# RetNet retention and a SwiGLU block on one core: later segments' retention in half chunks of 64 tokens instead of whole chunks of 128

## The chip, the core and the metric

The kernel runs on one core of a Trainium2 chip. TensorE (PE in the profile) multiplies into PSUM, which has eight banks here, each 128 partitions by 512 float32 columns. VectorE (DVE), ScalarE (ACT) and GpSimd (POOL) do the element-wise work, and SyncE (SP) issues nearly all DMAs in one ordered queue. The metric is the device time of one execution in microseconds (us). The kernel before took 665.63 us (median of 3 runs, 664.43 to 665.97).

## The reference

```python
q, k, v: (4, 8, 768, 64)            # batch, heads, sequence, head_dim
gamma = 1.0 - 2.0 ** (-5.0 - np.arange(H))
for t in range(S):
    state = gamma * state + einsum('bhd,bhe->bhde', k[:, :, t], v[:, :, t])
    y[:, :, t] = scale * einsum('bhd,bhde->bhe', q[:, :, t], state)
x = y.transpose(0, 2, 1, 3).reshape(B * S, H * D)       # 3072 x 512
g = x @ w_gate; silu = g / (1 + exp(-g)); val = x @ w_val
return (silu * val) @ w_out          # d_ff 1536, weights in float64 words
```

Retention is a recurrence over tokens with one 64x64 state for each head, and can be done by chunks. Inside a chunk, scores of key and query are multiplied by a table of decays and then by the values. What lies before the chunk enters as the query, scaled, times the state at the chunk's start. At the chunk's end the state is decayed and the scaled keys times the values are added.

## The kernel before

**Segments and stages.** The 24 chunks of 128 tokens (4 batches of 6) are worked through in four segments of six chunks. A segment has three pairs, the two chunks of a pair being at the same place in two batches. Each segment goes through an up stage (the gate and value products over 12 slices `f` of the hidden size) and a down stage (72 slots, six for each slice, of three matmuls each, `down`, L917). The first segment's retention stands at the start of the program, and its up stage is `up` (L692), in which the weights are also read from memory, converted from float64 words, split and stored for the later segments. The order of that work is written out by hand in two strings of tokens, `START` and `beside` (L299 and L306): `l` loads a chunk's part, `A` a part of the decay table, `s m o t` are the parts of retention, `U a b c S C T Z` the stages of one up weight, `F Z` those of one down weight, `P` a load for the next segment.

**Retention of segments 1 to 3** is put between the slots of the down stage before it (`down_stage`, L956). I call the three passes loop 1 (down stage of segment 0, in which segment 1's retention is computed) to loop 3. The table `PARTS` (L945 to L950) says before which slot a part of which pair comes. For each pair there are five visits: `s` for heads 0 to 3 and `s` for heads 4 to 7 (`scores_of`, L556), `m` (`mix_own`, L609), `o` (`mix_other`, L620) and `t` (`state2`, L652). The first pair has its two `s` in one visit, and the last chunk of a sequence has no `t`. All of these matmuls go through one helper, `mm` (L552), so the profile shows them as L552.

**How a pair lies on the array.** Every part but the state multiplies with 64 rows and 64 columns, so that four such matmuls have four different quarters of the array. For each head a chunk has three blocks of scores of its four: both halves of the queries against the first half of the keys as one matmul of 128 columns (`low`), and the second half of the queries against the second half of the keys as one of 64 (`high`). The state's matmuls use all 128 rows, 64 columns wide. In all a pair has 48 matmuls of 128 columns and 48 of 64.

**What stands beside it.** `decayed` (DVE) takes scores out of PSUM with the decay table (L574), `scale_q2` scales the queries in place (one chunk on DVE, the other on POOL, L628), `scale_k2` the keys (16 ACT instructions, L639, or POOL), `decay2` the old state (4 on ACT, L650), `keep_state` adds the new sum (L666), `bring_y` copies the result out of PSUM (8 on ACT, L805), and `make_x` splits it for the next up stage. Banks 6 and 7 (`R0`) hold scores, then results, then state sums of a pair, one after another.

**What sets the order.** Each engine's instructions stand in the order of planned times: `at(t, ...)` puts a step at a time, `run` sorts them. The times come from `COST`, from `PASS_U` and `PASS_D`, and from the table `WHEN` (L334), which holds an offset for each step. Loads for the coming retention are put at slots by `LOADS` (L953); `HOME` (L516) says which of five places of the tile `loads` each takes, and so on whose last reader each waits. `UNITS` puts the first up weights of the next segment into the same places.

Of the kernel before, what the change touches and what calls it, by code (L numbers as in the profile page):

```python
# [17 lines left out]
P = 128  # L18
# [31 lines left out]
def tile_retnet_swiglu(  # L50
# [203 lines left out]
    def sums_t(piece, parts=range(3)):  # L254
# [30 lines left out]
        "L": lambda n: load_side(n // 2, n % 2), "h": lambda n: high_side(n),  # L285
# [6 lines left out]
    def do(order):  # L292
        for o in order.split():
# [6 lines left out]
        l0:0 A1 l1:0 l0:3 A0 l0:2 l1:3 s0 l2:0 l2:1 A2 l1:2 l3:0 l3:1 l4:2 l4:0 l2:3 l2:2 s1  # L300
        l3:3 m0 l4:1 K0 U0:0 s2 l3:2 m1 k1 l5:0 Q2 l5:1 V0:0 x0:0 l5:2 t0 l4:3 s3 o2 q3 k2
        x0:1 t1 U1:2 g2 k3 m2 l5:3 a0:1 x0:2 t2 o3 s4 g3 x0:3 m3 x1:0 t3 b0:1 a0:0 c0:1 S0:1
        b0:0 s5 q4 S0:0 c0:0 q5 x1:1 o4 x1:2 x1:3 o5 m4 C0:1 m5 a1 x2:0 C0:0 b1 T0:0 p0 x2:1
        T0:1 T0:2 S1 p1 c1 x2:2 C1
    """
    beside = """  # L306
        U14:8 | x2:3 g4 | U2:0 | T1:0 U15:9 | T1:1 c2 a2 b2 | S2 C2 U3:4 |
        T2:0 U12:6 | g5 c12 U13:7 | T2:1 a3 Z0 a13 T1:2 | U5:0 a12 b3 M0 b12 | c3 S3 Z1 | C3
            T2:2 |
        U4:2 L0 L1 | S12 M1 a5 T3:0 | C12 | F12:0 a4 F12:1 | T3:1 L3 U6:4 b4 c4 S4 T3:2 | b5  # L310
            c6 C4 S5 F12:2 T4:0 |
         | c5 Z2 T4:1 | C5 a6 b13 M2 c13 | S13 a14 b6 T4:2 C13 | h0 Z3 T5:0 b14 T5:1 | S6
            F13:0 F13:1 U7:2 U16:6 U8:0 |
        M3 F12:3 | Z4 S14 T5:2 c7 | a7 F13:2 a15 C6 F13:3 | c14 Z12 b15 U17:7 U9:4 | Z13 b7
            C14 T6:0 F14:0 F14:1 T6:1 | T6:2 |
        S7 C7 | F14:2 a8 | S15 c15 b8 a16 F14:3 | C15 M4 | a17 c8 | F15:0 F15:1 |
        Z5 T7:0 S8 T7:1 C8 M5 b16 | U10:2 T7:2 L2 Z6 | U19:9 U11:0 S16 T8:0 a9 c16 | Z14
            U18:8 | F15:2 c17 | C16 b9 T8:1 F16:0 b17 h1 S9 |
        c9 F16:1 | T8:2 F16:2 C9 S17 | M6 F16:3 | F15:3 C17 T9:0 c10 P2 a10 | b10 U20:6 a18
            k4 F17:0 S10 a19 Z7 U21:7 | T9:1 Z15 F17:1 c18 |  # L320
        a11 M7 | F17:2 U23:5 C10 T9:2 | b18 S18 F17:3 Z9 | c11 b11 T10:0 T10:1 C18 b19 | P1
            F18:0 F18:1 c19 S19 S11 k5 | Z16 |
        a20 F18:2 Z8 a21 | t4 | C19 F18:3 C11 U22:4 c20 P0 M8 | b20 T11:0 F19:0 | b21 F19:1
            S21 T11:1 | T11:2 a23 S20 F19:2 a22 C20 |
        Z17 Z18 T10:2 M9 F20:0 F19:3 | b23 F20:1 c21 Z10 C21 F20:2 Z19 | b22 S22 c22 F21:0 |
            F20:3 S23 t5 c23 C22 | F22:0 | F21:1 Z20 C23 |
        Z11 | F23:0 F21:2 F22:1 F21:3 F22:2 M10 | F22:3 | Z22 F23:1 |  | F23:2 F23:3 |
# [26 lines left out]
        ('h', 6): (-7.31, -2.68, -1.02),  # L354
# [148 lines left out]
    def mix(c):  # L503
        vn, a = chunks[c][2], att.pop(c)
        y, own = y_parts(c)
        for k, (n, i, to) in enumerate(own):
# [7 lines left out]

    spots = [loads[:, ts(i, 512)] for i in range(10)]
    HOME = (2, 3, 4, 0, 1, 2, 3, 4, 0, 1, 4, 0)  # L516
    blocks = [loads[:, ds(i, UNIT)] for i in (2048, 2048 + UNIT, 0)]
    side = [t.rearrange("p (i t) -> p i t", i=2)
            for t in (tab[:, : 2 * TA], kept_vk.rearrange("p a b -> p (a b)")[:, : 2 * TA])]
    kdec_b = tab[:, ds(2 * TA, H)]  # L520
    half = [ds(0, D), ds(D, D)]
# [3 lines left out]
    def load_side(g, m):  # L525
        cols = decays[:, MASK0:QDEC0].rearrange("p (i g t) -> p i g t", i=2, g=2)[:, :, g]
        nc.sync.dma_start(out=side[g][half[m], :, : 2 * P], in_=cols[half[0]])
        if g == 0:
            nc.sync.dma_start(out=kdec_b[half[m]], in_=decays[half[1 - m], ds(KDEC0, H)])

    def high_side(g):

        low, high = (side[g][:, :, c].rearrange("p i (n t) -> p i n t", n=2)
                     for c in (ds(0, 2 * P), ds(2 * P, P)))
        for i in range(2):
            copy(high[:, i], low[:, i, :, :D])

    def load_pair(s, n):
        p, w = divmod(n, 4)
        w = (0, 1, 2, 3)[w]  # L540
        own = [spots[2 * HOME[n] + i] for i in range(2)]
        given.setdefault(p, {})[w] = own
        for i in range(2):
            src = (k_t, q_t, v_n, k_n)[w][seg_chunks(s)[2 * p + i]]
            if w < 2 or i == 0:
                nc.sync.dma_start(out=own[i], in_=src)
            else:
                for m in half:
                    nc.sync.dma_start(out=own[i][m], in_=src[half[m is half[0]]])
# [4 lines left out]
    score_banks = {}  # L554

    def scores_of(p, g, own=(R0, R0 + 1)):  # L556
        score_banks[p, g] = own = [banks[i] for i in own]
        kt, qt = ([pairs(t) for t in given[p][w]] for w in range(2))
        for b in range(2):
            for m in range(2):  # L560
                for r in range(2):
                    x, n = half[r], 2 * g + b
                    mm(own[r][half[m], ts(b, P)], kt[m][x, n, half[0]],
                       qt[m][x, n], b == 0)
        for b in range(2):
            for m in range(2):
                for r in range(2):
                    x, n = half[r], 2 * g + b
                    mm(own[r][half[m], ds(2 * P + D * b, D)],
                       kt[1 - m][x, n, half[1]], qt[1 - m][x, n, half[1]])  # L570

    def decayed(p, g, i):
        att[p, g, i] = tmp[:, ts(2 * g + i, TA)]
        tt(att[p, g, i], score_banks[p, g][i][:, :TA], side[g][:, i], op=mul)  # L574
# [7 lines left out]
    def old(s, p, other):  # L582
        for b in range(2):
            for h in range(2):
                for r in range(2):
                    c, n = (1 - r if other else r), 2 * h + b
                    mm(y_of(n, r, c), state_of(seg_chunks(s)[2 * p + c], 1)[half[r], n],
                       pairs(given[p][1][c])[half[r], n], b == 0 and not other)

    def low(p, first):  # L590
        for i in range(2):
            for b in range(2):
                for h in range(2):
                    for r in range(2):
                        n = 2 * h + b
                        mm(y_of(n, i, r), given[p][2][r][half[r], ts(2 * n + i, D)],
                           att[p, h, i][half[r], ts(b, P)], first and i == b == 0)

    def high(p):
        for i in range(2):  # L600
            for b in range(2):
                for h in range(2):
                    for r in range(2):
                        n = 2 * h + b
                        mm(y_of(n, i, 1 - r, half[1]),
                           given[p][2][1 - r][half[r], ts(2 * n + i, D)],
                           att[p, h, i][half[r], ds(2 * P + D * b, D)])

    def mix_own(s, p):  # L609
        ci = seg_chunks(s)[2 * p] % NCK  # L610
        if ci:
            old(s, p, False)
        low(p, ci == 0)
# [6 lines left out]
    def mix_other(s, p):  # L620
        high(p)
        if seg_chunks(s)[2 * p] % NCK:
            old(s, p, True)

    def scale_q2(p, i):
        t = pairs(given[p][1][i])
        if i:
            pool(t, t, qdec, op=mul)  # L628
        else:
            both(t, t, qdec, mul)  # L630

    def scale_k2(p, i):
        kd = given[p][3][i].rearrange("p (h d) -> p h d", h=H)
        dec = kdec_b if i else kdec
        if p == 2 and i == 0:
            pool(kd, kd, dec[:, :, None].to_broadcast([P, H, D]), op=mul)
            return
        for h in range(H):
            act(kd[:, h], kd[:, h], AF.Copy, scale=dec[:, ds(h, 1)])  # L639

    def new_states(s, p):
        ci = seg_chunks(s)[2 * p] % NCK
        new, was = (states[:, (ci + o) % 2] for o in range(2))
        return ci, new, was, banks[R0].rearrange("p (c n e) -> p c n e", c=2, n=NP)

    def decay2(s, p):
        ci, new, was, st = new_states(s, p)
        if ci:
            for n in range(NP):
                act(new[:, :, n], was[:, :, n], AF.Copy, scale=gdec[:, ds(n, 1)])  # L650

    def state2(s, p):  # L652
        ci, new, was, st = new_states(s, p)
        for c in range(2):
            vn, kd = given[p][2][c], given[p][3][c]
            for n in range(NP):
                for i in range(2):
                    h = ts(2 * n + i, D)
                    mm(st[half[i], c, n], kd[:, h], vn[:, h], c == n == 0)

    def keep_state(s, p):
        ci, new, was, st = new_states(s, p)
        if ci == 0:
            copy(new, st)
        else:
            tt(new, new, st, op=add)  # L666
# [278 lines left out]
    CYCLE = [("s", 0, 0), ("s", 1, 4), ("m", 0, 9), ("o", 0, 12), ("t", 0, 16)]  # L945
    STARTS = (2, 22, 41)
    PARTS = {}
    for p, b in enumerate(STARTS):
# [167 lines left out]
```

## Time and profile before

| what | us |
|---|---|
| median of three runs | 665.63 |
| the profiled execution, its own time | 665.63 |
| its span, first to last instruction | 663.8 |
| start, before the first up-stage matmul | 0 to 27 |
| up stage of segment 0 | 27 to 140 |
| loop 1, 2, 3 (down stage with the next segment's retention) | 140 to 209, 297 to 366, 454 to 521 |
| up stages of segments 1, 2, 3 | 209 to 297, 366 to 454, 521 to 607 |
| last down stage, no retention | 610 to 657 |

The profile is one execution. Where a matmul of float32 is recorded it stands as two records, so "x32" of L552 is 16 matmuls. Busy time of an engine is the union of its instructions. The chain of waits goes back from the last instruction to what released it each time; a piece of it is one line of the program that ran without a wait.

### The profile page before, as it was taken

The numbers are of one execution on the slowest core, as the hardware profiler recorded it, in microseconds if no ns is written. First come the engines' busy times: TensorE is split into PE (matmuls) and PEld (weight loads), VectorE is DVE, ScalarE is ACT, GpSimd is POOL, SyncE is SP. The second block draws the span as 40 slices with busy tenths as digits, with TensorE's granted clock in tenths as the row PEclk, the third lists the DMA queues.
The fourth block names the chain that finished last, engine by engine and source line by source line (L and its number), as shares of the span: only waits on it lengthen the run. The fifth ranks groups of instructions, "written<-read, shape, count | busy, mean of one in ns | idle before, by whom it ended". The sixth has DMA issues, their size and how long they took to land.

```text
span 663.8 us, 12360 instructions
## 1 busy us (share of the span) xinstructions
PE 653.1 (98%) x4712; PEld 546.9 (82%) x4712; DVE 468.5 (71%) x741; ACT 386.8 (58%) x792; POOL 252.9 (38%) x166
## 2 busy tenths in 40 slices
PE   8999999999999999999999999999999999999997
PEld 7755555567778999997777999998777999999886
DVE  4667999996768666666778666667776776668541
ACT  1788888656846555555648655555574655654221
POOL 2444657620105655640112655661000656652000
PEclk9999999999999999999999999999999999999999
DMA  9999998877675533456684534365766454323553
GB/s 334 343 361 315 335 369 338 320 263 272 214 216 211 186 115 144 161 174 204 236 259 162 206 117 144 106 215 191 238 216 235 152 180 149 112 91 109 190 191 142
DMA packets 48459, 141.32 MB, mean 213 GB/s; under 512 B 4752, under 2 KB 17808, under 8 KB 48400
## 3 DMA queue, kind: packets, MB, share of 16 engines
q1 hardware_dynamic: 47968, 139.88, 60.9%
q8 instruction: 37, 0.61, 0.4%
q10 hardware_dynamic: 432, 0.66, 0.3%
q14 instruction: 22, 0.18, 0.1%
HBM read 113.78 MB, written 26.74 MB: 212 GB/s over the span
## 4 chain that ended last, share of the span: by engine, by line
PE 87%; DMA 8%; DVE 3%; issue 1%; ACT 0%; SPq 0%; POOL 0%; ACTq 0%; DVEq 0%
PE bank L870 39%; PE bank L920 31%; PE bank L699 9%; PE bank L552 7%; DMA rawp<-in_w_gate_dram 2%; DMA wup<-first 2%; DMA rawp<-in_w_val_dram 1%; DMA hT<-in_v_n_dram 1%; DMA hT<-in_q_t_dram 1%; DMA tab<-in_decays_dram 1%; DVE first L80 1%; PE bank L507 0%; DVE first L231 0%; DMA out_dram<-chunk_x 0%; PE bank L500 0%
## 5 line engine op out<-in xcount | busy, mean ns | idle before, releaser
L870 PE MATMUL bank<-x,gitem 128*128 128x384 f32 x1296 | 231.5, 335 | 0.0
L870 PEld LDWEIGHTS bank<-x,gitem 128*128 128x128 f32 x1296 | 226.0, 188 | 0.5
L920 PE MATMUL bank<-oitem,gitem 128*128 128x512 f32 x864 | 214.0, 401 | 0.3 <-DVE hT L888 0.3
L920 PEld LDWEIGHTS bank<-oitem,gitem 128*128 128x128 f32 x864 | 159.0, 188 | 40.9 <-issue 2.9
L770 POOL TENSOR_TENSOR gitem<-gitem 128x768 fp32r<-128x768 f32 x72 | 138.2, 1942 | 113.9 <-DVE gitem L767 109.4
L699 PE MATMUL bank<-first 128*128 128x384 f32 x336 | 111.0, 489 | 2.5 <-ACT tmp L720 1.5
L699 PEld LDWEIGHTS bank<-first 128*128 128x128 f32 x336 | 62.6, 190 | 49.1 <-ACT tmp L733 2.9
L764 ACT ACTIVATE gitem<-loads 128x768 fp32r<-128x768 f32 x72 | 57.9, 840 | 36.0 <-issue 30.7
L628 POOL TENSOR_TENSOR loads<-loads,tab 128x512 f32<-128x512 f32 x8 | 12.7, 1588 | 140.7 <-PE bank L552 140.7
L767 DVE SCALAR_TENSOR_TENSOR gitem<-gitem,loads 128x768 fp32r<-128x768 f32 x72 | 65.5, 951 | 0.0
L764 ACT ACTIVATE gitem<-hT 128x768 fp32r<-128x768 f32 x48 | 40.1, 839 | 38.7 <-PE bank L920 25.2
L767 DVE SCALAR_TENSOR_TENSOR gitem<-gitem,hT 128x768 fp32r<-128x768 f32 x48 | 45.5, 952 | 18.9 <-ACT gitem L764 18.9
L237 POOL TENSOR_TENSOR first<-first,rawp 128x1024 int32<-128x1024 int32 (+1 forms) x21 | 41.2, 1971 | 33.2 <-ACT rawp L224 14.1
L80 DVE SCALAR_TENSOR_TENSOR gitem<-gitem 128x768 fp32r<-128x768 f32 x48 | 46.1, 965 | 0.9
L886 ACT COPY tmp<-bank 128x384 f32<-128x384 f32 x36 | 17.3, 480 | 46.2 <-PE bank L870 44.5
L870 PE MATMUL bank<-x,oitem 128*128 128x384 f32 x216 | 43.8, 338 | 0.0
L805 ACT COPY chunk_x<-bank 64x256 f32<-64x256 f32 x72 | 25.5, 367 | 29.5 <-PE bank L552 28.8
L770 POOL TENSOR_TENSOR oitem<-oitem 128x256 fp32r<-128x256 f32 x36 | 28.6, 794 | 29.7 <-DVE oitem L767 27.4
L887 DVE TENSOR_TENSOR hT<-bank,tmp 128x384 f32<-128x384 f32 x36 | 20.1, 557 | 26.9 <-PE bank L870 26.9
L889 DVE TENSOR_TENSOR hT<-hT,bank 128x384 f32<-128x384 f32 x36 | 19.9, 553 | 26.9 <-ACT bank L889 26.9
L870 PEld LDWEIGHTS bank<-x,oitem 128*128 128x128 f32 x216 | 38.1, 188 | 0.0
L885 DVE TENSOR_TENSOR tmp<-bank,tmp 128x384 f32<-128x384 f32 x36 | 20.0, 557 | 19.3 <-PE bank L870 19.3
(99 smaller groups left out, 728.1 us busy)
## 6 DMA issues: line engine op xcount, KB each, us to landing
oitem<-wdnt SPq DMA_DIRECT2D x45, 768.0 KB, 4.3
loads<-wup SPq DMA_DIRECT2D x36, 896.0 KB, 4.9
wup<-first SPq DMA_DIRECT2D x12, 896.0 KB, 8.0
wdnt<-oitem SPq DMA_DIRECT2D x12, 768.0 KB, 5.9
rawp<-in_w_gate_dram SPq DMA_DIRECT2D x12, 512.0 KB, 7.7
rawp<-in_w_val_dram SPq DMA_DIRECT2D x12, 512.0 KB, 6.9
out_dram<-chunk_x SPq DMA_DIRECT2D x23, 256.0 KB, 2.3
loads<-in_q_t_dram SPq DMA_DIRECT2D x18, 256.0 KB, 3.8
```

The source lines that it names most:

```text
L80: stt(o, x, 1.0, y, op0=mul, op1=op)
L237: pool(d.bitcast(I32), d.bitcast(I32), lo.bitcast(I32), op=add)
L552: nc.tensor.matmul(o, a, b, start=start, stop=True, skip_group_check=True)
L699: nc.tensor.matmul(o, w[:, slot, k], a[:, KH - 1 - k], start=(start and k == 0), stop=(stop and k == KH - 1), skip_group_check=True)
L764: act(o[0], x, AF.Copy, scale=CUT / FAR)
L767: stt(o[1], f32(o[0]), -FAR, x, op0=mul, op1=add)
L770: op(o[2], f32(o[0]), f32(o[1]), op=add)
L805: copy(cx[half[i], ds(2 * h, 2), c], y_both(h, i, c))
L870: nc.tensor.matmul(o, w[:, a, k], xs_of[s][:, a, OP[p], KH - 1 - k], start=start and a == k == 0, stop=a == 2 and k == KH - 1, skip_group_ ...
L885: steps = (lambda: copy(p1, x), lambda: tt(c11, z, p1, op=add), lambda: act(gate, c11, AF.Silu, scale=ONE), lambda: copy(u2, x), lambda: c ...
L887: lambda: copy(p5, wb), lambda: tt(h1, x, p5, op=add),
L920: nc.tensor.matmul(banks[tok], hs[f][:, a, ds(i * TH + u * P, P)], wo[f][:, a], start=f == a == 0, stop=f == NF - 1 and a == 2, skip_group ...
```

## The change

Retention of segments 1 to 3 is done in half chunks of 64 tokens. Only the two diagonal blocks of scores are computed, each 64 by 64. The second half of a chunk sees the first one through a state in the middle of the chunk (`mids`): the old state times the decay over 64 tokens plus the sum over the first half. The state at the end is the middle one, decayed over 64, plus the sum over the second half (`next_state`). So a pair's state is computed before its results, and a pair has four visits of 32 matmuls of 64 columns each: `t`, `s`, `m`, `o`. The first pair has `t` and `s` in one visit before slot 2, with the sums in banks 4 and 5 (4 and 3 in the first loop) and the scores in banks 6 and 7. For a sequence's first chunk the part with the old state falls away, and for its last chunk only the middle state is computed.

The keys of the first pair are now scaled before the down stage begins; a scaling instruction covers both chunks of a pair (8 of 128x128). Loads get new slots and places (`PLACES`). The decay table for the blocks is loaded in two DMAs of 64x8x64 elements instead of four of 64x2x256, and `g64`, the decay over 64 tokens, is made by one ACT instruction. The strings `START` and `beside` are written anew for the first segment and its up stage: the same conversions, stores and loads in another order, with the keys of the second chunk scaled on DVE instead of POOL, and with one more load for segment 1 in them (`P3`).

```diff
-        "L": lambda n: load_side(n // 2, n % 2), "h": lambda n: high_side(n),
+        "L": lambda n: load_side(n), "h": lambda n: decay_64(n),
     START = """
-        l0:0 A1 l1:0 l0:3 A0 l0:2 l1:3 s0 l2:0 l2:1 A2 l1:2 l3:0 l3:1 l4:2 l4:0 l2:3 l2:2 s1
+        l0:0 l0:2 l1:0 A0 A1 A2 l1:2 l0:3 l2:1 l2:0 l1:3 s0 l2:2 l3:0 l3:1 l5:2 l3:3 l2:3
...
-    HOME = (2, 3, 4, 0, 1, 2, 3, 4, 0, 1, 4, 0)
+    PLACES = [(0, 0, 4), (0, 2, 3), (0, 3, 2), (0, 1, 0), (1, 3, 1), (1, 2, 2), (1, 0, 4), (1, 1, 3),
+              (2, 3, 0), (2, 2, 1), (2, 0, 4), (2, 1, 0)]
...
+    def scores_of(p):
+        for c in range(2):
+            for n in range(NP):
+                for e in range(2):
+                    for r in range(2):
+                        mm(banks[R0 + r][half[c ^ e], ts(c * NP + n, D)],
+                           kt[c][half[r], n, half[e]], qt[c][half[r], n, half[e]], c == n == 0)
...
     def old(s, p, other):
+        for e in range(int(cs[0] % NCK == 0), 2):
+            for b in range(2):
+                for h in range(2):
+                    for r in range(2):
+                        c, n = (1 - r if other else r), 2 * h + b
+                        st = mids[p % 2][:, c] if e else state_of(cs[c], 1)
+                        mm(y_of(n, r, c, half[e]), st[half[r], n],
+                           pairs(given[p][1][c])[half[r], n, half[e]])
...
     def mix_own(s, p):
-        ci = seg_chunks(s)[2 * p] % NCK
-        if ci:
-            old(s, p, False)
-        low(p, ci == 0)
+        own_half(p, 0)
+        old(s, p, False)
...
     def decay2(s, p):
-                act(new[:, :, n], was[:, :, n], AF.Copy, scale=gdec[:, ds(n, 1)])
+                act(mid[:, :, n], was[:, :, n], AF.Copy, scale=g64[:, ds(n, 1)])
...
+    def keep_state(s, p, c):
+        if ci == 0:
+            nc.vector.tensor_copy(mid[:, c], sum_of(p, c, 0))
+        else:
+            tt(mid[:, c], mid[:, c], sum_of(p, c, 0), op=add)
+        if ci < NCK - 1:
+            copy(new[:, c], sum_of(p, c, 1))
+
+    def next_state(s, p):
+        if ci < NCK - 1:
+            for n in range(NP):
+                stt(new[:, :, n], mid[:, :, n], g64[:, ds(n, 1)], new[:, :, n], op0=mul, op1=add)
...
-    CYCLE = [("s", 0, 0), ("s", 1, 4), ("m", 0, 9), ("o", 0, 12), ("t", 0, 16)]
-    STARTS = (2, 22, 41)
-    COST = {"s": 1.0, "m": 1.3, "o": 1.1, "t": 0.8}
-    LOADS = {5: 7, 6: 15, 7: 19, 8: 19, 9: 27, 10: 39, 11: 46}
+    PARTS = {2: "s0", 8: "m0", 11: "o0", 19: "t1", 23: "s1", 29: "m1", 32: "o1",
+             39: "t2", 45: "s2", 50: "m2", 53: "o2"}
+    SCALES = {1: 16, 2: 30}
+    COST = 1.2
+    LOADS = {5: 4, 6: 5, 7: 12, 8: 13, 9: 20, 10: 25, 11: 38}
...
             for n in range(5):
-                at(t - (18, 13, 12, 5, 4)[n], load_pair, s + 1, n)
+                at(t - (13, 12, 18, 5, 4)[n], load_pair, s + 1, n)
+            for h in range(H):
+                at(t - 12 + 1.0 * h, scale_k2, 0, [h])
+            at(t - 8.0, decay2, s + 1, 0)
```

## The prediction

> **What bounds the kernel now.** First the page's busy times and its chain shares.
>
> ```profile
> PE 653.1 (98%) x4712; PEld 546.9 (82%) x4712; DVE 468.5 (71%) x741; ACT 386.8 (58%) x792; POOL 252.9 (38%) x166
> PE 87%; DMA 8%; DVE 3%; issue 1%; ACT 0%; SPq 0%; POOL 0%; ACTq 0%; DVEq 0%
> ```
>
> PE is busy 98% of the span and is 87% of the chain. So work taken from PE shortens the run, unless something else is then late. Where that could be, the stages tell (stretch, length, busy time of PE, weight load, DVE, ACT, POOL, granted clock, DMA share, GB/s):
>
> ```profile
> 27.00:140.30 113.30, 110.81 (x369) 63.28 (x366) 100.54 (x158) 91.63 (x165) 62.84 (x38) 1.00 0.93 332
> 140.30:209.10 68.80, 68.80 (x765) 53.34 (x765) 52.71 (x86) 42.05 (x100) 8.10 (x4) 1.00 0.69 238
> 209.10:297.00 87.90, 87.90 (x506) 87.79 (x505) 59.47 (x96) 48.85 (x95) 52.52 (x36) 1.00 0.47 161
> ```
>
> In the first up stage DVE is at 89% and DMA at 93% too: its order is tight on all sides. In loop 1 PE never rests, while DVE has 16 us to spare. There the chain, in order of time, prices each visit of retention (start, us, what). First loop 1's first pair and the beginning of its second, then pieces of loop 2, then the last down stage.
>
> ```profile
> 142.98 1.50 PE bank L552 x64
> 144.47 6.50 PE bank L920 x27
> 150.97 1.47 PE bank L552 x48
> 152.44 2.29 PE bank L920 x9
> 154.74 1.06 PE bank L552 x48
> 155.80 3.00 PE bank L920 x12
> 158.80 1.08 PE bank L552 x32
> 159.88 3.00 PE bank L920 x12
> 162.88 0.83 PE bank L552 x32
> ...
> 306.44 1.03 PE bank L552 x32
> ...
> 309.77 0.62 PE bank L552 x32
> ...
> 353.21 0.86 issue
> 354.08 1.15 PE bank L552 x32
> ...
> 610.16 47.17 PE bank L920 x201
> ```
>
> **Prices of a matmul and of a visit.** Two records are one matmul. `mix_own` is 24 of 128 columns (1.47); without the old state it is 16 (1.03): 0.44 / 8 = 0.055 us for one, and 1.03 - 16 x 0.055 = 0.15 to begin a visit. The `high` part alone is 16 of 64 columns (0.62): (0.62 - 0.15) / 16 = 0.0294. Check: the first pair's scores, 16 of each, 0.15 + 0.88 + 0.47 = 1.50, as the chain has it. A visit also costs the down stage: between two visits 12 records take 3.00, while the undisturbed last stage runs 201 in 47.17, or 12 in 2.82. That is 0.18 more for each visit.
>
> **Part 1, the matmuls.** A visit of 32 is 0.15 + 32 x 0.0294 = 1.09, the joint one of 64 is 2.03, and one of 24 (first chunk of a sequence) 0.86. The last chunk's state sums only the first half: 16 matmuls that use one row half at a time, two at a time like today's state, so I take that row, 1.08.
> - Loops 1 and 3: 2.03 + 2 x 1.09 (first pair), 4 x 1.09 (second), 1.08 + 3 x 1.09 (third) = 12.9. Before, the chain's thirteen pieces add up to 14.57. Gain 1.65 each.
> - Loop 2: 2.03 + 2 x 0.86, 4.36, 4.36 = 12.5, before 14.84. Gain 2.37.
> - Sum -5.7. Bounds: if the new orders (rows outside columns in the state) shared the array less well, the states would pay, seven of 32 at double price, 7 x 32 x 0.0294 = +6.6; no row speaks for less than 0.0294.
>
> A rule speaks against the whole: the Trainium skill, "TensorE: Matmul & The Clock Gate", section "Wait — 56ns, not 53.3ns?", says that matmul starts are never closer than about 25 ns however narrow. Then 1104 matmuls of two records would cost 55 us against 33 by the row, and the run would be some 16 us slower, near 682. The row has 32 records in 0.62, 19 ns each, with four matmuls on four quarters; it decides.
>
> **Part 2, fewer visits.** 13 + 14 + 13 = 40 become 33: 7 x 0.18 = -1.3. (The 0.15 is in the sums above.)
>
> **Part 3, the stall in loop 2.** PE waited 0.86 at 353.21, before the third pair's state. ACT had sat 8.4 us for that pair's keys (until 347.33), so that its copies out of the result banks ran till 353.98. Those keys are now loaded at slot 13 instead of 46, and the state comes before its results: -0.9 (bounds -0.9 and 0).
>
> **Part 4, element-wise work, off the path.** For each pair on DVE: four score evacuations of 0.55 become two of 0.68 (row of 128x512), one of 0.68 for the state becomes two of 0.41, and `next_state` adds four, priced by the nearest row of 128x256 at 0.42 or less: 3.7 becomes 4.1 to 4.6, which DVE's 16 us in a loop cover. ACT: 16 key instructions (3.93) become 8 of 128x128 (by the row of four in 1.26, 2.5), plus two copies of 0.38. POOL's 1.59 for queries becomes two of 0.79 (row of 128x256).
>
> **Part 5, where a wait may come.**
> - *Second pair's scores* (slot 23). They need banks 6 and 7 free of the state sums of slot 19, and both of ACT's copies out stand behind, after `o` of the first pair: 8 result copies 3.03, keys 2.5, splits 0.92 and 1.07, old state 1.26, one split of the hidden slice 0.84, one 0.42, the copies 0.75: 10.8. PE gets there in 8 downs (5.8), the state 1.09, 4 downs (3.0): 9.9. A wait of 0.9, or none if ACT overlaps them as its rows do (0.29 for a 0.39 instruction). Also behind ACT's copy: DVE's second state sum, and with it the score evacuation. I take 0.5 in each loop, +1.5 (0 to 2.7).
> - *Third pair's queries* take the keys' place, so their DMA starts after the state at slot 39, and the scores stand at slot 45: 6 downs, 4.4 us. Two DMAs, 0.4 to issue each; q landings in loops 1 and 2 took 3.9 and 3.5. Just in time: 0. Upper bound from the load's row, all landings:
>
> ```profile
> DMA to landing us min/median/max: 2.5/3.7/10.7
> ```
>
>   Behind it on SP stand a down weight and the first up weight; both have over 5 us.
> - *Keys of the first pair* are scaled on ACT before loop 1, with the old state 3.8 us. ACT idles 4.24 there (138.0 to 142.3, waiting for PE), so 0; without that cover PE waits up to 3.8. In the up stages before loops 2 and 3 they stand singly between copies that PE needs, which have some 0.4 us of slack (1.05 for a product, 0.48 a copy, 0.17 to start). Before loop 3 three of them, 1.0, and the old state, 1.26, come in a row where ACT idled 1.29, so the next copy is about 0.6 late: +0.5 (0 to 1.2). Their DMAs go first in the queue now, three issues instead of two (1.6 us against 1.2); the up weight behind has 8 us or more.
>
> **Part 6, the first segment's new order.** The same work, otherwise placed. SP's queue of loads: the last value of chunk 3 (20.70 us, at the chain's head) moves from 24th to 22nd among blocks of 256 KB that land every 0.76 (347 GB/s), 1.5 earlier; but chunk 4's values stay 29th, and the chain score, result, score, result of chunks 4 and 5 is then the end: first up product 0 to 0.6 earlier. In the stage, PE idles 1.46 + 0.69 + 0.35 = 2.5 in all: that is the most to win. The most to lose: the same again, and 0.5 MB more to load at 332 GB/s (1.6): +4.1. The small tables: 1024 packets of 256 B replace 512 of 1 KB (46 ns): 0.6 to 3.0 us of 16 queues by the rows of 32 B and 1 KB, for 1.5 before, inside that bound. I take 0.
>
> **The sum.** 663.8 - 5.7 - 1.3 - 0.9 + 1.5 + 0.5 = 657.9 of span. 1.8 lies outside the span (665.6 - 663.8), and the profiled execution's own time is the median of the runs: **659.7 us**.
>
> **The rivals.**
> 1. *ACT's handover decides.* The wait at the second pair is its full 0.9 or more, and the third pair, in loop 2 with the same copies, and the first pair, whose sums ACT and DVE take out in turn, get one like it: three waits of 0.9 in three loops, 8.1 instead of 1.5, so 666. For it: the stall at 353.21 was of this kind. Against: ACT has 25 us free in a loop.
> 2. *The third pair's queries come late*, the slower side. If they land in 10.7 instead of 3.7, PE waits 6.3 at slot 45 in each loop: +19, near 679. It decides from 6.8 us to landing (three waits of 2.4 bring 659.7 above 667). For it: one place is used twice, with a transfer of 768 KB issued right after. Against: the median, and that the queries go first.
> 3. *The first segment's order is worse on the chip*: +4.1, 664. For it: three engines at 80 to 98% there. Or better: -2.5, 657.
> 4. *The narrow matmuls do not share the array*: each costs double, 1104 x 0.0294 = +32, near 692. Against: the row of 0.62.
>
> **How the numbers follow.** Chances: the forecast, with the small spread of its waits, 0.60; better, with the idle time of the first stage gone too, 0.06; rival 1 0.10; rival 3's loss 0.13; rival 2 0.09; rival 4 0.02. A difference under 0.2% (1.3 us) cannot be told from none. Faster than 664.3: forecast, better, half of rival 1 and most of rival 3, 0.81; within, 0.07; slower, 0.12. The forecast's own range is 656.5 to 662.5. The low end adds the gain of rival 3 and no new wait: 659.7 - 2.0 - 2.5 = 655.2. The high end takes in rivals 1 and 3: 666.
>
> **What would show it.** In the profile after: L552's visits of 64 records at 1.1 and one of 128 at 2.0 in each loop; loops of some 66 us; no piece "issue" in them; before the second pair's scores a wait for ACT's copy of at most 0.9; the first up stage ending within 2.5 us of 140. The prediction is wrong if PE waits at slot 45 for a load, if visits are 1.3 or longer, or if the first down matmul comes after 144.

## The result, and the profile after

The changed kernel took 669.49 us (median of 20 runs, 668.43 to 670.85), the kernel before 665.80 beside it (20 runs, 664.43 to 669.33): a ratio of 1.005, 95% interval 1.0039 to 1.0061. It is slower, where 659.7 was forecast. The profiled execution of the changed kernel took 668.43, with a span of 666.6 (663.8 before).

Lines are numbered anew: 698 is the first up stage's product, 869 the later ones', 919 `down`, 554 `mm`, 568 `decayed`, 621 `scale_k2`, 613 `scale_q2` on POOL, 657 and 659 `keep_state` on DVE and ACT, 665 `next_state`, 763, 766 and 80 (or POOL's 769) the three steps of splitting a hidden slice or a weight, 804 `bring_y`, 772, 80, 778 and 784 the four steps of `make_x`. In the experiments with the old strings they are one higher, in e8 those from 657 on three lower. An evacuation below is `decayed` taking scores out of PSUM, an x step is a step of `make_x`, a split is a step of 763, 766 or 80, and a slot is three down matmuls.

The page of the changed kernel first, its busy times and the shares of the chain:

```profile
PE 649.5 (97%) x5288; PEld 544.4 (82%) x5288; DVE 471.4 (71%) x774; ACT 387.1 (58%) x778; POOL 259.3 (39%) x174
PE 70%; DVE 9%; ACT 8%; DMA 6%; issue 3%; POOL 3%; SPq 1%; DVEq 0%; ACTq 0%; POOLq 0%
```

PE has 3.6 us less to do than before (653.1), yet the span is 2.8 longer, so PE waits 6.4 us more. The chain says for whom: PE's share fell from 87% to 70%, and DVE, ACT and POOL together rose from 3% to 20%. By stage (stretch, length, busy PE, weight load, DVE, ACT, POOL, granted clock, DMA share, GB/s):

```profile
27.80:142.20 114.40, 110.32 (x367) 63.65 (x366) 94.28 (x158) 92.70 (x172) 63.52 (x38) 1.00 0.92 335
142.20:211.20 69.00, 67.31 (x957) 52.63 (x957) 54.73 (x94) 40.95 (x92) 9.33 (x7) 1.00 0.65 225
211.20:299.50 88.30, 88.22 (x506) 87.71 (x505) 59.81 (x97) 51.18 (x103) 52.94 (x36) 1.00 0.48 160
```

In the first up stage PE rests 4.1 us (2.5 before), in loop 1 it rests 1.7 (0 before). The clock is the same. DVE has 2.0 us more to do in the loop and ACT 1.1 less: 55 and 41 of 69 us, so neither is full. The list of PE's waits in loop 1 is short:

```profile
PE bank L919 <- DVE gitem L80: 0.8, 1, 0.8
PE bank L554 <- DVE tmp L568: 0.7, 1, 0.7
PE bank L554 <- ACT states L659: 0.3, 1, 0.3
```

At the beginning of each later up stage PE's weight loads wait for POOL as well, 0.4 each (us in all, times, longest); the list before the change has no such wait:

```profile
PEld bank L869 <- POOL gitem L769: 1.2, 3, 0.4
```

The three in the loop belong to the second pair. Here PE's own row (start, us, what, and in brackets the rest before it and who ended it): the second pair's scores, `m` cut in two, and the slot after `o`.

```profile
165.91 1.33 PE L554 MATMUL bank<-loads 64*64 64x64 f32 x64 [0.25 <-ACT states L659]
...
171.58 0.33 PE L554 MATMUL bank<-tmp,loads 64*64 64x64 f32 x2
172.58 0.63 PE L554 MATMUL bank<-tmp,loads 64*64 64x64 f32 x27 [0.68 <-DVE tmp L568]
...
181.34 1.90 PE L919 MATMUL bank<-oitem,gitem 128*128 128x512 f32 x7 [0.77 <-DVE gitem L80]
```

`m` begins at 171.58 and the next down matmul comes at 173.66: 2.08 instead of 1.09, so its wait costs 1.0 with the halt inside. The scores lose 0.42 (a wait of 0.25, and a visit of 1.26, from 165.91 to 167.17, instead of 1.09), the slot 0.77: 2.2 us. Loops 2 and 3 show the same three. The chain of waits of loop 1 (start, us, what) leads back to their cause:

```profile
144.88 2.02 PE bank L554 x128
...
151.30 1.09 PE bank L554 x64
...
154.68 1.16 PE bank L554 x64
...
158.88 2.32 ACT loads L621 x8
...
164.15 0.73 ACT gitem L763
164.88 0.31 ACT x L784
165.19 0.02 issue
165.21 0.38 ACT states L659
...
167.09 0.68 DVE x L778
167.77 2.02 DVE states L665 x4
169.79 0.87 DVE gitem L766
170.66 0.60 DVE tmp L568
171.25 0.67 DVE loads L80 x2
171.92 0.60 DVE tmp L568
172.52 0.87 DVE gitem L80
173.39 1.14 DVE x L778
...
175.52 0.83 ACT gitem L763
176.35 0.88 ACT loads L621 x4
177.23 0.20 issue
177.43 1.27 ACT loads L621 x4
178.69 0.75 ACT gitem L763
```

Read downwards it is one thread that never lies on PE from 155.8 to 181.3. After `o` of the first pair ACT copies the results, scales the second pair's keys, splits, and copies the states (165.21). DVE goes on with x, then with the four `next_state` (2.02), then with a split, and only then with the evacuation that `m` waits for. Behind that comes the x step of 1.14, on which ACT waits in order (6.12 idle before L784); behind L784 stand a split, the third pair's keys and the split that the down matmul wants.

The visits themselves are as cheap as forecast (1.09, and 2.02 for the joint one; those with the old state left out 0.86 and 0.93). The first matmul of each stage, taken from the timelines, gives this account:

| stretch, us | before | after | e3 | e6 | e11 |
|---|---|---|---|---|---|
| start | 27.1 | 27.8 | 28.0 | 27.1 | 27.0 |
| first up stage | 112.7 | 113.9 | 114.6 | 114.3 | 111.8 |
| loop 1 | 69.2 | 69.4 | 68.0 | 67.9 | 67.3 |
| up stage 1 | 87.9 | 88.3 | 88.3 | 88.2 | 87.8 |
| loop 2 | 68.9 | 67.8 | 66.0 | 65.7 | 65.6 |
| up stage 2 | 87.8 | 88.7 | 88.7 | 88.7 | 87.8 |
| loop 3 | 67.6 | 67.8 | 66.4 | 65.8 | 65.8 |
| up stage 3 | 87.8 | 88.1 | 88.2 | 88.2 | 87.8 |
| last down stage | 54.8 | 54.8 | 54.8 | 54.8 | 54.8 |

(e3, e6 and e11 are experiments, below.) Three places lose: the loops, which gain 0.7 in all instead of some 6; the up stages, 1.6 longer, of which the wait for POOL makes 1.2; the first segment, 1.9 longer. The last figure is a difference of two single profiles, and the first segment varies from profile to profile: with both strings new it takes 141.7 to 143.6 in five kernels (the changed one, e2, e3, e4, e8; mean 143.0), with both old 139.8 to 141.9 in five (before, e1, e6, e7, e9; mean 141.1).

### The profile page after: what moved, and what is told of

The parts are those of the page before. It is cut to its first block, busy times and chain, and to the rows that moved or that the text cites. A ratio compares the mean times of both kernels' runs of the same rounds, so it can differ in the third digit from the quotient of the medians.

```text
span 666.6 us, 13548 instructions
## 1 busy us (share of the span) xinstructions
PE 649.5 (97%) x5288; PEld 544.4 (82%) x5288; DVE 471.4 (71%) x774; ACT 387.1 (58%) x778; POOL 259.3 (39%) x174
## 4 chain that ended last, share of the span: by engine, by line
PE 70%; DVE 9%; ACT 8%; DMA 6%; issue 3%; POOL 3%; SPq 1%; DVEq 0%; ACTq 0%; POOLq 0%
PE bank L869 39%; PE bank L919 16%; PE bank L698 10%; PE bank L554 4%; ACT chunk_x L804 2%; ACT loads L621 2%; DMA rawp<-in_w_gate_dram 2%; DVE gitem L766 2%; POOL gitem L769 2%; ACT gitem L763 1%; DVE gitem L80 1%; DMA wdnt<-oitem 1%; DMA hT<-in_v_n_dram 1%; DVE x L778 1%; DVE x L80 1%
## 5 line engine op out<-in xcount | busy, mean ns | idle before, releaser
L769 POOL TENSOR_TENSOR gitem<-gitem 128x768 fp32r<-128x768 f32 x72 | 140.1, 1968 | 111.6 <-DVE gitem L766 106.4
L613 POOL TENSOR_TENSOR loads<-loads,tab 128x256 f32<-128x256 f32 x18 | 20.2, 1143 | 140.5 <-PE bank L554 140.5
L766 DVE SCALAR_TENSOR_TENSOR gitem<-gitem,loads 128x768 fp32r<-128x768 f32 x72 | 65.6, 951 | 0.0
L784 ACT ACTIVATE x<-x 128x256 fp32r<-128x256 f32 (+2 forms) x27 | 18.8, 696 | 35.4 <-DVE x L778 35.4
```

What stands on the lines that cost most here:

```text
L613: pool(t[:, :, e], t[:, :, e], qdec[:, :, :D], op=mul)
L766: stt(o[1], f32(o[0]), -FAR, x, op0=mul, op1=add)
L769: op(o[2], f32(o[0]), f32(o[1]), op=add)
```

## The experiments

The theory (A): the forecast's savings on PE are all there; about 2 us a loop are lost because DVE and ACT do their work at the second pair in an unlucky order, and about 2 us by the new order of the first segment. Rivals: (B) the first segment alone, (C) the half chunks themselves. Runs that were made together share a chip, and chips differ (the kernel before took 666.3 to 666.7 on these), so ratios to the kernel before are compared; the changed kernel's is 1.005, from its own 20 runs, and it was not run again beside the experiments.

| run | median us | ratio to before, 95% |
|---|---|---|
| changed kernel | 669.49 | 1.0050 (1.0039 to 1.0061) |
| e1 old first segment | 668.29 | 1.0021 (1.0002 to 1.0041) |
| e2 new first segment, old retention | 668.85 | 1.0027 (1.0008 to 1.0047) |
| e3 next_state late | 664.92 | 0.9972 (0.9953 to 0.9990) |
| e4 third keys earlier | 666.47 | 0.9996 (0.9976 to 1.0015) |
| e6 all three | 661.76 | 0.9921 (0.9900 to 0.9942) |
| e7 handover | 661.69 | 0.9920 (0.9902 to 0.9938) |
| e8 queries on DVE | 669.25 (one run) | |
| e9 first split on DVE | 659.55 | 0.9902 (0.9879 to 0.9926) |
| e10 old START, new beside | 666.86 | 1.0007 (0.9993 to 1.0021) |
| e11 all | 658.78 | 0.9876 (0.9852 to 0.9899) |
| e12 one load swapped | 668.10 | 1.0023 (1.0008 to 1.0038) |

**e1 and e2: the first segment's order, undone and alone.**

```diff
 (e1) changed kernel, START and beside of the kernel before, with
-        ... U22:4 c20 P0 M8
+        ... U22:4 c20 P0 P3 M8
 (e2) kernel before, START and beside of the change, with
-    for n in range(3, 5):
-        at(end + 1.0 + n, load_pair, 1, n)
+    at(end + 5.0, load_pair, 1, 4)
```

> Half chunks as in the change, but START and beside as before (P3 beside P0). Theory (A) two parts: the first segment's new order costs what the profiles show at its end (142.19 against 140.29, 1.9 us) and the rest is lost at the second pair of each loop: then this is 1.9 below the changed kernel, about 667.6 (666.6 to 668.4), and still above the kernel before (665.8). Rival (B), the first segment's order alone costs the time and the loops gain as forecast: 669.5 - 3.7 or lower, at or under 665.8. Rival (C), the half chunks alone cost it and the order is worth nothing: 669.5.

> Whole chunks as before, with START and beside of the change (P3 leaves the list of loads after the stage). (A): 1.9 above the kernel before, 667.7 (666.8 to 668.6). (B): 669.5 or more. (C): 665.8, no difference.

Undoing it took 0.29% off (1.9 us), doing it alone put 0.27% on (1.8 us), each known to about 0.2% (1.3 us). Both as (A) has it. (B) falls: with the old order the changed kernel is still slower than before, if only just (1.0002 at the least). (C) alone falls too: the order costs something without any half chunk.

**e3: next_state behind the evacuations.**

```diff
-                    at(t + 2.5, next_state, nxt, p)
+                    at(t + (2.5 if n == 2 else 9.0), next_state, nxt, p)
```

> The changed kernel with next_state of the second and third pair put 9.0 instead of 2.5 after its visit, so behind both score evacuations on DVE. (A), the four next_state (2.02 in the profile after) stand ahead of the evacuation that m1 waits for: the wait of 0.69 and the slow visit (2.08 instead of 1.09) at the second pair go, 1.0 a loop, and next_state takes 1.4 for four as it does where POOL rests: 666.5 (666 to 667.5). (C), narrow visits themselves are slow: m1 stays at 2.08 and the time at 669.5.

The ratio fell by 0.0078, some 5 us, and the kernel is now faster than before. Expected were 3. PE's row in loop 1 shows why it was more:

```profile
172.50 0.69 PE L554 MATMUL bank<-tmp,loads 64*64 64x64 f32 x32
173.01 0.41 PE L554 MATMUL bank<-loads,states 64*64 64x64 f32 x16
173.25 0.41 PE L554 MATMUL bank<-loads,tmp 64*64 64x64 f32 x16
...
180.80 1.90 PE L919 MATMUL bank<-oitem,gitem 128*128 128x512 f32 x7 [0.30 <-DVE gitem L80]
```

`m` runs through from 172.50 to 173.59 (1.09), and the slot waits 0.30 instead of 0.77, since the x step of 1.14 comes earlier too. One move, two waits: 1.47 a loop, 4.4 in three, and the three loops are 4.6 shorter in the table. The visits were not slow for themselves, so (C) falls here as well.

**e4: the third pair's keys earlier on ACT.**

```diff
-    SCALES = {1: 16, 2: 30}
+    SCALES = {1: 16, 2: 24}
```

> The changed kernel with the third pair's keys scaled at slot 24 instead of 30, so that on ACT they stand before the copy that waits 6.12 for DVE. (A), ACT waits in order for DVE there and everything behind is late: the wait of a down matmul for DVE's split (0.77 in each loop, 2.3 in the page) goes, 667.2 (666.8 to 668.2), m1 unchanged. (C): 669.5.

0.9996: 0.54% under the changed kernel, where 2.3 us (0.35%) were expected; the intervals allow either. The slot's wait is gone in all three loops, and `m` is unchanged (0.70 waited). In the profile loops 1 and 2 are 1.0 and 1.3 shorter, loop 3 not: PE halts for 0.7 in the middle of the first pair's `o` (467.6 to 468.3), which the profile puts down to nothing it shows. That one stays open.

**e8: POOL out of the way of next_state.** Scaling both chunks' queries on DVE.

```diff
             for e in range(2):
-                if i:
-                    pool(t[:, :, e], t[:, :, e], qdec[:, :, :D], op=mul)
-                else:
-                    both(t[:, :, e], t[:, :, e], qdec[:, :, :D], mul)
+                both(t[:, :, e], t[:, :, e], qdec[:, :, :D], mul)
```

> The changed kernel with both chunks' queries scaled on DVE, POOL out of the loops' middle. If next_state takes 0.58 and more for one because POOL works beside it: 0.34 for each here, four in 1.36 instead of 2.02, and the same everywhere. If it is slow for itself (its operands, their place): 2.02 again. m1 still waits behind next_state, for DVE has two operations of 0.34 more between the two evacuations, which take what the faster next_state gives: 0.69 to 0.8 as before, and the time within 1 us of the changed kernel's.

The durations of the second pair's `next_state` (min/median/max in ns), in the changed kernel, where POOL scales queries from 167.34 on beside it:

```profile
L665 DVE SCALAR_TENSOR_TENSOR states<-tmp,tab,states x12: 337/580/835, 167.7 to 482.0; 128x128 f32<-128x128 f32 x12
```

then in e8, where POOL does not work in the loop's middle:

```profile
L662 DVE SCALAR_TENSOR_TENSOR states<-tmp,tab,states x12: 341/344/346, 169.5 to 482.2; 128x128 f32<-128x128 f32 x12
```

So it is POOL beside it, not the operation: four take 1.05 in the chain of e8 (they overlap a little) instead of 2.02. e3 agrees: with `next_state` moved away it is a split of DVE (128x768) that runs beside POOL there, and it takes 1.49 instead of 0.95. Half of my expectation was wrong: `m` does not wait any more, as the 1.0 that is saved lies ahead of its evacuations and the two added query steps lie behind them. But those push the x step back, and the slot's wait grows from 0.77 to 1.4. The three loops together take 204.2 instead of 205.0, and the time of the one run is the changed kernel's. Most of the loss moved along the same thread.

**e6: e1, e3 and e4 in one.**

> The old first segment, the late next_state and the earlier third keys in one kernel. (A): what was seen singly adds up except for the down matmul's wait, of which the late next_state has already taken two thirds (0.9 of 2.3 left): 664.9 - 1.2 - 0.9 = 662.8 (661.8 to 664), below the kernel before by some 0.5%. If the three gains were one and the same wait seen thrice: 664.9, as with the late next_state alone.

0.9921, 661.76, just under the range: the three gains add up but for the overlap, and this kernel is 0.8% faster than before. The table has the loops at 67.9, 65.7 and 65.8.

**e7: three more steps moved.**

```diff
-        ('w', 0, 0): (-11.39, -6.27, -4.75),
+        ('w', 0, 0): (-11.39, -8.0, -7.0),
-                        at(t + 0.1 * (1 + c), keep_state, nxt, p, c)
+                        at(t + 0.1 * (1 + c) - (1.2 if n == 19 else 0), keep_state, nxt, p, c)
-            at(t - 8.0, decay2, s + 1, 0)
+            at(t - 2.5, decay2, s + 1, 0)
```

> The same, and three more steps moved in their engine's order: the second pair's state copies on ACT ahead of a hidden split (L660, the wait of 0.25 and the slow visit of 1.27 at slot 23), DVE's step of the first up weight of the next segment ahead of the last x steps (POOL ends its split 0.4 after PE wants it at the end of each loop), and before loop 3 the old state's four decays into ACT's idle time of 2.9 after its last copy. (A), these are the waits that are left: 3 x 0.45 + 3 x 0.4 + 0.5 = 3.0 off, 659.8 (659 to 661.5), where the forecast for the change stood. If PE's work and not order sets it by now: 662.8.

A miss: 0.9920, no gain that the runs can tell. The states' wait went (0.8 in all), but 0.5 of waits for the evacuation behind it came; the span shrank by 0.8. The wait for POOL stayed at 0.41 in each loop, though POOL began 2.8 earlier. POOL's step in e6 (start, us, in brackets its rest before):

```profile
206.29 3.90 POOL L770 TENSOR_TENSOR gitem<-gitem 128x768 fp32r<-128x768 f32 x1 [17.17 <-DVE gitem L767]
```

and in e7:

```profile
203.49 6.25 POOL L770 TENSOR_TENSOR gitem<-gitem 128x768 fp32r<-128x768 f32 x1 [14.30 <-DVE gitem L767]
```

It began 2.80 earlier and took 2.35 longer. DVE's row beside it in e7 ends with these two:

```profile
206.81 1.21 DVE L779 SCALAR_TENSOR_TENSOR x<-x 128x1024 fp32r<-128x1024 f32 x1
207.94 1.28 DVE L938 TENSOR_SCALAR chunk_x<-bank 128x512 f32<-128x512 f32 x2
```

In the up stages POOL's operation takes 1.85 (median), where DVE rests or mostly reads PSUM, and up to 2.4 where one of DVE's two-operand splits falls beside it. Here DVE goes without a pause through steps that read two operands outside PSUM, L779 as the last; POOL ends (209.74) 1.80 after L938 has begun, which reads PSUM. In e6 L938 begins at 208.40 and POOL ends at 210.19, 1.79 later; before the change 207.79 and 209.57, 1.78. That is POOL's whole 1.85 each time, within 0.1: by these rows it gets nothing done until DVE's row is through, however early it is started.

**e9: that step on DVE.**

```diff
-        at(t + c, lambda: near_c(it["o"][0]))
+        at(t + c, lambda: near_c(it["o"][0], both if (f, g) == (0, 0) else pool))
```

> The kernel of e7 with the last step of the next segment's first up weight on DVE instead of POOL. In e7 POOL's step began 4.1 us earlier and ended when DVE's row of work ended all the same (6.25 us long instead of 3.91), so PE still waited 0.41. If POOL gets on only where DVE rests, taking the step to DVE (0.95) ends it some 3 us before PE wants it: 0.4 off at each of three loop ends, 660.5 (659.8 to 661.3). If PE waits there for something else (the last x step): 661.7 as before.

659.55, just under the range. (The 4.1 us there count from e3, where POOL began at 207.58; from e6 to e7 it is 2.80.) The ratios of e7 and e9 alone, 0.9920 and 0.9902, have intervals that overlap; the profiles show the gain in its place: no wait for POOL is left, and the three up stages in which it stood take 263.6 instead of 265.0. The step in e9, on DVE, is done at 207.23, 2.3 before PE's first up product at 209.5:

```profile
206.28 0.95 DVE L80 SCALAR_TENSOR_TENSOR gitem<-gitem 128x768 fp32r<-128x768 f32 x1
```

**e10 and e12: what in the first segment's order.** e10 keeps the new `beside` under the old `START`; e12 exchanges two words in the new one.

```diff
 (e12)
-        T0:1 x2:1 b1 p1 U2:0 x2:2 U14:8
+        T0:1 x2:1 b1 p1 U14:8 U2:0 x2:2
```

> The changed kernel with START of the kernel before and beside of the change (what the one has done already is left out of the other; the second chunk's keys on POOL again). If the order before the first up product costs the 2 us of the first segment: 1.002 of the kernel before, like e1. If it is the order in the up stage: 1.005 like the changed kernel.

> The changed kernel with two neighbours in START exchanged: U14:8, a load whose place is free, ahead of U2:0, which waits for a buffer. In the trace after SP sits on U2:0 from 21.1 to 28.68 with U14:8 behind it, and DMAs move 235 GB/s in 24 to 28 where e10 (U14:8 issued at 21.62) has 348. If that is what the first segment's order costs: like e10, 1.000 to 1.003 of the kernel before, some 2 us under the changed kernel. If it is the order of the first loads or the second chunk's keys on DVE: 1.005 as the changed kernel.

e10 stands at 1.0007: it is `START` that costs, and the new `beside` is not worse than the old one. SP's queue in the changed kernel (start, us, what):

```profile
20.72 0.38 SPq L194 DMA_DIRECT2D rawp<-in_w_gate_dram  x1
28.68 0.37 SPq L194 DMA_DIRECT2D rawp<-in_w_val_dram  x1
29.09 0.51 SPq L194 DMA_DIRECT2D rawp<-in_w_gate_dram  x1
29.64 0.50 SPq L194 DMA_DIRECT2D loads<-in_w_out_dram  x1
```

and what moves from 24 to 33 (columns as in the stages above, the last two the DMA's share and GB/s):

```profile
24.00:28.00 4.00, 4.00 (x63) 3.54 (x62) 3.54 (x8) 2.15 (x5) 1.92 (x2) 1.00 0.72 235
28.00:33.00 5.00, 5.00 (x16) 2.94 (x16) 4.03 (x9) 4.82 (x9) 0.69 (x2) 1.00 0.66 211
```

The same two views of e10:

```profile
21.62 0.44 SPq L194 DMA_DIRECT2D loads<-in_w_out_dram  x1
27.62 0.38 SPq L194 DMA_DIRECT2D rawp<-in_w_val_dram  x1
```

```profile
24.00:28.00 4.00, 4.00 (x62) 3.40 (x57) 2.96 (x6) 3.26 (x6) 2.56 (x2) 1.00 1.00 348
28.00:33.00 5.00, 5.00 (x17) 2.91 (x16) 4.44 (x10) 4.72 (x10) 0.91 (x1) 1.00 0.86 284
```

The load into `loads` (`U14:8`) has a free place. In the old order it goes out at 21.6 and keeps the DMA engines busy while SP sits on the next buffer of `rawp`. In the new order that buffer's load is ahead of it in the one queue, SP sits on it until 28.68, and the DMA engines move 235 GB/s instead of 348. All five kernels with the new `START` as it was (the changed one, e2, e3, e4, e8) have 235 to 253 there, all others 343 to 353. The exchange alone (e12) stands at 1.0023: 0.27% off, 1.8 us, inside what was expected. It brings the rate back in 24 to 28, as its stretches show, and gives a part of it back in 28 to 33 (161 against 211):

```profile
24.00:28.00 4.00, 3.89 (x56) 3.40 (x58) 3.97 (x9) 1.92 (x4) 1.30 (x1) 1.00 1.03 349
28.00:33.00 5.00, 5.00 (x27) 3.11 (x23) 3.60 (x10) 4.68 (x8) 1.28 (x1) 1.00 0.50 161
```

Rate times length, from 24 to 33 e12 moves 2.20 MB, the changed kernel 1.99 and e10 2.81: the exchange restores a quarter of what was missing there. So its 1.8 us (1.2 either way) rest on the run times alone, and something more in `START`, the other loads' order or the second chunk's keys on DVE, may account for the distance to e10 (0.16%), which the intervals cannot tell from none. Nor does a single profile size it: with the same old strings the first up stage took 112.6 in e1 and 114.3 in e6.

**e11: e9 with e10's strings.**

> The kernel of e9 with e10's strings (START as before, beside of the change) in place of both strings as before. e10 stood 0.14% under e1, inside their intervals: 658.6 if that is real, 659.5 if not; 0.988 to 0.991 of the kernel before.

658.78, 0.9876: 1.2% faster than the kernel before, at the low end of what was expected. Its page:

```profile
PE 646.3 (99%) x5288; PEld 544.1 (83%) x5288; DVE 475.8 (73%) x776; ACT 387.6 (59%) x778; POOL 249.2 (38%) x172
PE 78%; DMA 8%; ACT 6%; DVE 5%; issue 2%; SPq 1%; POOL 1%; ACTq 0%; POOLq 0%; DVEq 0%
```

From the first loop on, PE waits 0.5 us in all. Of the 8.1 us by which its span is shorter than the kernel's before (655.7 against 663.8), 7.0 lie in the three loops. The half chunks were a gain; the rest of their change gave it away.

## Why the prediction was wrong, point by point

**Parts 1 to 3 nearly held.** Visits cost 1.09 and 2.02 as worked out; only the last chunk's state, taken at 1.08, is 0.91. Between visits 18 down matmuls take 4.40 against 4.22 undisturbed: the 0.18 of a visit. The stall of loop 2 is gone. Together they were to take 7.9 off the loops; with the waits removed (e11) the loops are 198.7 against 205.7, 7.0 off. The floor of about 25 ns between matmul starts, which the Trainium skill states in "TensorE: Matmul & The Clock Gate", section "Wait — 56ns, not 53.3ns?", does not show here either: 64 records in 1.09 are 17 ns each.

**Part 4 is the step that failed first**, where it says that 4.1 to 4.6 us of DVE work a pair are covered by "DVE's 16 us in a loop". The free time is there (14 of 69 us after). But DVE takes its steps in one order, and `next_state`, which PE needs only at the next pair, stood just ahead of the evacuation that PE needs next. Its price was off besides: "0.42 or less" each, measured 0.34 alone and up to 0.835 beside POOL. What it cost is the wait of `m`, 1.0 a loop, and by delaying the x step part of the slot's 0.77: late `next_state` (e3) took 1.47 a loop off. I priced POOL's queries and DVE's states in neighbouring sentences and never asked whether they run at the same time.

**Part 5 was too small, and stopped too early.** The second pair's scores, which I took at 0.5 a loop, lose 0.42. But I followed ACT's handover to the evacuation and not on to `m`, which waits for it, nor to the x step and the down matmul behind: 1.0 and 0.77 more. In three loops 1.5 was taken and 6.6 measured. The end of each loop, where POOL's split is late by 0.4 (1.2 in all), is nowhere in it: in loop 1 it ends 0.90 after the first up product begins (211.14), before the change 0.61 after (208.96), where PE did not wait; why it shifted is not shown. The keys in the up stages were right: 0.5 taken, up stages 1 and 2 are 0.2 and 0.6 longer than up stage 3, which has none. The third pair's queries, taken at 0, cost nothing: no wait at slot 45.

**Part 6, taken at 0, cost 1.8 to 1.9** by e1 and e2. e10 puts it on `START`, and the run times of e12 put most of it on one load's place in SP's queue, though the bytes moved show that place mending only a part. I counted the chunks' loads in that queue by their places and did not look at the weights' loads, which wait for buffers and hold what is behind them.

Of the distance of 8.7 between the forecast span (657.9) and the profiled one (666.6) the second pair makes 5.1, the first segment 1.9, the loops' ends 1.2; the last 0.5 is not traced, and lies within what Parts 1 to 3 were too large by (7.9 against 7.0).

**The rivals.** Rival 1, at 666, had the right size and in part the right kind: ACT's late handover itself is 0.42 of the 2.2 a loop, the rest is DVE's order behind it. It looked for more waits of the kind it knew, at three pairs, and not for what stands behind the first; that its 8.1 lies near the 6.6 measured is luck. Rival 3's loss came too, at half its size. I gave them chances as if only one could be true, so the range ended at 666; both losses came, and together with the loops' ends they are the result. Rivals 2 and 4 did not happen. Of the signs that I named for a wrong prediction none came true (no wait at slot 45, visits at 1.09, first down matmul at 141.7), which shows that they watched the wrong places; of those for a right one, the loops of some 66 us failed at once (69.4, 67.8, 67.8).

The median of the 20 runs lies 1.1 above the profiled execution, which was the fastest of them; that completes the 9.8 between 659.7 and 669.49, and it is not explained.

## What to carry to other kernels

Free time of an engine covers added work only where that work stands in the engine's order behind what the bounding engine wants next. So for each added step, list what is queued behind it until the next thing PE waits for, and go on from that wait to the one after it. In an order written out by hand, a change that makes one engine faster needs the others' order redone: the same half chunks were 0.5% slower or 1.2% faster by the order of the steps around them and one step's engine. In an ordered DMA queue, put a load whose place is free ahead of one that waits for its buffer; here that brought 349 GB/s instead of 235 while the other waited.

## What was not expected of the hardware

DVE and POOL hold each other up, both ways. A DVE step over 128x128 took 0.34 with POOL at rest and up to 0.835 beside POOL's query scaling. POOL's step over 128x768 took 1.85 (median) in the up stages and 3.90 and 6.25 at the loops' ends, ending each time 1.8 after DVE's row of two-operand steps. The Trainium skill, "SBUF — State Buffer", section "Who interferes with whom", says that a DVE instruction with two inputs there contends with a GpSimd instruction that reads there, and calls the lock on the shared ports exclusive. That they contend agrees with these rows. POOL's rows look exclusive too; DVE's do not show it, as four steps lost 0.97 in the 1.43 that they ran beside POOL (167.69 to 169.12). What the rows add is that a POOL step that waits is not let in between two DVE steps: in e7 five that began after it went past it.
